# Banded attention into a softplus MLP on one core: q loaded as six tokens per partition, the picks and casts moved in the order of work

## The chip, the cores and the metric

The kernel runs on one core of one Trainium2 chip. The metric is the time of one execution on the device, in microseconds; the kernel before takes 512.18 us (median of three runs, 511.51 to 513.37).

The core's engines each run their own queue strictly in order: PE (matrix products), DVE and ACT (vector and scalar work; both read PE's results in PSUM), POOL (elementwise work that cannot read PSUM), and SP, which here only issues DMAs. An instruction waits at the head of its queue until what it needs is ready, and everything behind it waits too.

## The reference

Eight batches, eight heads, 576 tokens, head size 64. Attention with a band of 32 tokens to each side, plus eight global tokens that see everything and are seen by everyone; then an MLP with softplus.

```python
scores = scale * np.matmul(q, k.transpose(0, 1, 3, 2))
mask = np.abs(pos[:, None] - pos[None, :]) <= 32
mask = mask | is_global[:, None] | is_global[None, :]
attn = softmax(np.where(mask, scores, -1e9))          # over the last axis
x = np.matmul(attn, v)                                # -> (4608 tokens, 512)
out = softplus(x @ w_in) @ w_out                      # w_in 512 x 2048, w_out 2048 x 512
```

## The kernel before, in words

**Blocks and steps.** Heads go in pairs (p = 0 to 3), so that two heads of 64 fill 128 partitions. Queries go in blocks of 64 tokens: nine blocks a batch, 72 in all (n). A block's keys are the 128 positions around it and the eight global columns, 136 in all. The main loop runs over steps s; in step s the scores of block s are made, while older blocks are in later stages. Steps 0 to 9 ("P") hold attention alone. From step 10 on eight steps make a period: four "B" steps (s mod 8 = 2 to 5) carry the first MLP product h of 512 tokens, four products to each of 16 output tiles; four "A" steps carry the second product, o. Both are cut into four quarters a step (`moe(0)` to `moe(3)`), and attention work is put between the quarters. Tables filled ahead of the loop say which block is in which stage in which step: E (exponentials), M (sum and normalisation), TP (transpose of the probabilities), PGT (transpose of the global columns), VV (value product), TU (turns), CA (casts of q and k), SV (casts of v), G1 to G3 (rows of the global queries). The order in the code is the order in each queue; no planner changes it.

**One block.** `s_pe` (L344) makes scores in PSUM; `s_max` (L355, DVE) adds the mask, writes them to SBUF negated and takes the row's minimum; `s_sub` (L360, POOL) subtracts it; `expo` (L364, ACT); `total` (L368 to L371) sums on DVE, takes the reciprocal and, on POOL, multiplies by 0 for rows that are global queries; `norm` (L379, L380, POOL) multiplies the 512 band columns and the 32 global columns in two instructions; `pt_pe` and `pt_ev` (L387 to L395) transpose; `pg_pe` (L400, L403) transposes the global columns of four blocks at once and copies them into R; `v_pe` (L413, L415) multiplies by v and by the global rows and leaves the result in xT, half by DVE (L421) and half by ACT (L422).

**Turns.** q and k arrive with tokens on the partitions. POOL casts them to bf16 (`cast`, L234). A turn multiplies by a unit matrix on PE (L251), five products of 128 tokens and eight extra columns that pick the global tokens out, in two parts of three and two (SPLIT). ACT evicts q in two halves, one for each head (L261 for the first two batches, L264 after), into qz; DVE evicts k into kx (L271). Then the "picks": DVE reduces the global columns of q to qg (L267) and of k (L277, L278), and POOL copies the kx blocks that start at an odd 64 (L273, L274).

**Loads.** SP issues q, k and v through eight stage buffers, in the order in which they are cast; a cast gives its buffer to the next load. Each of q, k and v of a pair takes four DMAs in pieces of 256 bytes (L156, L161). vB is a copy of v moved by 64 tokens (L239, L240), also on SP's queue, as are the stores of the results (L447).

**Ahead of the loop** stand constants (identity, masks, one-hot rows; L173 to L221, L463 to L519), the turns of batch 0 and its global rows. One of the constants, the eight indices, is spread over the partitions by POOL (L189). POOL also issues the loads of the weights (L522, L524).

The products of block 0 need all turns of batch 0 and `globals1` to `globals3`; a turn needs its cast. In step s of the kernel before, casts are at the step's end, one step ahead of the turn.

Of the kernel before, what the change touches and what calls it, by code (L numbers as in the profile page):

```python
# [13 lines left out]
FP32 = mybir.dt.float32  # L14
# [4 lines left out]
def kernel(  # L19
# [24 lines left out]
    EXT = P + NG  # L44
    KD = d_model // P
# [21 lines left out]

    def bank(shape, dt, name):
        return psa.tile(shape, dt, tag="a", name=name)
# [5 lines left out]
    stage = [const([P, NT5, P], FP32, f"stage{i}") for i in range(NSTG)]  # L75
# [8 lines left out]
    R = [[const([P, P], BF16, f"R{i}_{j}") for j in range(NJ)] for i in range(2)]  # L84
# [36 lines left out]
    for b in range(1, B):  # L121
        lo = 9 * (b - 1)
        ok = [s for s in range(lo, lo + 9) if kind[s] == "B"][:HP] if b > 1 else [1, 3, 5, 7]
        for p, s in enumerate(ok):
            TU[s].append((b, p))
            CA[s - 1].append((b, p)) if s > 0 else None
# [7 lines left out]
        assert max(g2 + 1, vs + 1) <= vslot[9 * b]  # L134


    order = [(0, w, p) for p in range(HP) for w in range(2)] + [(0, 2, p) for p in range(HP)]
    for s in range(NS):
        order += [(b, w, p) for b, p in CA[s] for w in range(2)] + [(b, 2, p) for b in SV[s] for p in range(HP)]
# [4 lines left out]
    def load_next():  # L144
        if loaded[0] == len(order):
            return
        b, w, p = order[loaded[0]]
        st = stage[loaded[0] % NSTG]
        loaded[0] += 1
        src = (q, k, v)[w]  # L150
        off = 0 if w == 0 else WIN
        for t0, t1 in ((0, 1), (1, NT5 - 1), (NT5 - 1, NT5)):
            lo, hi = max(0, t0 * P - off), min(S, t1 * P - off)
            p0 = lo - (t0 * P - off)
            if t1 - t0 == 1:
                nc.sync.dma_start(  # L156
                    out=st[p0:p0 + hi - lo, t0, :].rearrange("p (h d) -> p h d", h=2),
                    in_=src[b, 2 * p:2 * p + 2, lo:hi, :].rearrange("h s d -> s h d"))
            else:
                for h in range(2):  # L160
                    nc.sync.dma_start(  # L161
                        out=st[:, t0:t1, h * D:(h + 1) * D],
                        in_=src[b, 2 * p + h, lo:hi, :].rearrange("(t s) d -> s t d", s=P))

    gi_dram = global_idx.rearrange("(n one) -> n one", one=1).bitcast(I32)
    gi = const([1, NG], I32, "gi")
# [8 lines left out]
    ident = const([P, P], FP32, "ident")  # L175
# [3 lines left out]
    def iota(shape, pattern, base, mult, name):  # L179
        i = const(shape, I32, name + "_i")  # L180
        G_.iota(i[:], pattern=pattern, base=base, channel_multiplier=mult)
        return i, const(shape, FP32, name)

    posA_i, posA = iota([P, NT5], [[P, NT5]], -WIN, 1, "posA")
    posQ_i, posQ = iota([P, NT5], [[P, NT5]], 0, 1, "posQ")
    gf1 = const([1, NG], FP32, "gf1")
    V_.tensor_copy(gf1[:], gi[:])
    gf = const([P, NG], FP32, "gf")
    G_.partition_broadcast(gf[:], gf1[:1, :], channels=P)  # L189
    lower = const([P, NG, NG], FP32, "lower")  # L190
# [9 lines left out]
    rhsQ = const([P, NT5, EXT], BF16, "rhsQ")  # L200
    for rhs in (rhsQ, rhsA):
        V_.tensor_copy(rhs[:, :, 0:P], ident[:].unsqueeze(1).to_broadcast([P, NT5, P]))

    hsel = const([P, 2], FP32, "hsel")
# [7 lines left out]
    same = const([P, NG, NG], FP32, "same")  # L212
# [3 lines left out]
    dup = const([P, NG], FP32, "dup")  # L216
    V_.reduce_max(out=dup[:], in_=same[:], axis=AX.X)
    gs = const([P, NG], FP32, "gs")
    V_.scalar_tensor_tensor(out=gs[:], in0=dup[:], scalar=16384.0, in1=gf[:], op0=OP.mult, op1=OP.add)
    for pos, rhs in ((posQ, rhsQ), (posA, rhsA)):  # L220
# [417 lines left out]
```

## Time and profile before

| | us |
|---|---|
| median of three runs | 512.18 |
| profiled execution | 508.42 |
| its span, first to last instruction | 506.7 |
| PE busy in the span | 388.2 |
| ACT / POOL / DVE busy | 311.9 / 286.7 / 251.1 |

A row of groups in the profile reads: line, engine, operation, what is written <- what is read, shape, count, then busy time in us and mean ns of one, then the idle time of the engine ahead of these instructions and what ended it. A row of waits reads: who waited <- for whom, total us, times, longest. A timeline row has start and duration in us, and in brackets the idle time just before. A number of us after a window (A:B) is the busy time of one engine in it.

### The profile page before, as it was taken

Reading aid. Unit: us, or ns where it says so; the run is one execution under the profiler, and the core shown is the slowest. Engines: PE = TensorE matmul, PEld = TensorE weight load, DVE = VectorE, ACT = ScalarE, POOL = GpSimd, SP = SyncE. Lnnn points to the kernel's source line nnn. Section 1 sums busy time; section 2 is a strip of 40 time slices with the busy share of each in tenths; the row PEclk is TensorE's granted clock in tenths of the full one; section 3 lists DMA queues with packets and bytes.
Section 4 is the critical chain, followed back from the end, with each engine's and each line's share of the span. In section 5 each row is a group of like instructions: output and inputs, shape, how many; then the busy total and the mean of one; then the engine's idle time right before and its main releaser. Section 6 shows DMA issues by size and latency. Waiting matters only on the chain.

```text
span 506.7 us, 8834 instructions
## 1 busy us (share of the span) xinstructions
PE 388.2 (77%) x2746; PEld 222.0 (44%) x2795; DVE 251.1 (50%) x1124; ACT 311.9 (62%) x628; POOL 286.7 (57%) x477
## 2 busy tenths in 40 slices
PE   0124445567987898789987979797979789999996
PEld 0112234434554455445544645463446345545542
DVE  3653745553664475447546645663465356526100
ACT  1242545467848675886876588476837685776741
POOL 1338885745595468559756853794279448437000
PEclk9999999599999999999999999898989899999999
DMA  4542997544246324441651364125512401101102
GB/s 105 131 108 64 206 208 150 128 114 100 63 114 152 88 55 115 130 96 43 167 125 49 85 159 96 42 68 133 119 43 66 111 1 43 43 1 41 43 7 77
DMA packets 125950, 46.72 MB, mean 92 GB/s; under 512 B 117712, under 2 KB 119760, under 8 KB 125904
## 3 DMA queue, kind: packets, MB, share of 16 engines
q1 hardware_dynamic: 123216, 41.97, 34.0%
q0 software_dynamic: 2688, 4.19, 4.5%
q8 instruction: 22, 0.36, 0.3%
q14 instruction: 24, 0.20, 0.1%
HBM read 36.70 MB, written 9.44 MB: 91 GB/s over the span
## 4 chain that ended last, share of the span: by engine, by line
PE 36%; POOL 16%; issue 13%; ACT 11%; DVE 9%; SPq 9%; DMA 5%; POOLq 1%; ACTq 0%
PE o L441 14%; PE h L433 10%; SPq L161 5%; SPq L156 4%; POOL st L360 3%; ACT qz L264 3%; PE xo L415 3%; PE xo L413 3%; POOL vA L231 3%; DVE st L355 3%; POOL qn L234 3%; ACT g L436 2%; DMA vB<-vA 2%; POOL pn L379 2%; PE pt L387 2%
## 5 line engine op out<-in xcount | busy, mean ns | idle before, releaser
L433 PE MATMUL h<-xT,win 128*128 128x512 bf16 x552 | 144.2, 387 | 8.0 <-ACT xT L422 6.3
L441 PE MATMUL o<-wout,g 128*128 128x512 bf16 x552 | 139.7, 384 | 1.2
L360 POOL TENSOR_TENSOR st<-st,nb 128x544 f32<-128x544 f32 x72 | 78.8, 1095 | 60.3 <-DVE nb L355 60.2
L436 ACT ACTIVATE g<-h 128x512 bf16<-128x512 f32 x144 | 82.7, 597 | 20.5 <-PE h L433 18.7
L355 DVE CUSTOM_DVE_ANT_0 st<-s,mask 128x136 f32<-128x136 f32 x288 | 68.7, 293 | 19.5 <-PE s L344 19.1
L379 POOL TENSOR_TENSOR pn<-st,rs 128x512 bf16<-128x512 f32 x72 | 74.8, 1039 | 6.0
L433 PEld LDWEIGHTS <-win 128*128 128x128 bf16 x576 | 53.6, 100 | 51.1 <-issue 10.4
L251 PE MATMUL turn<-rhsQ,qn 128*128 128x136 bf16 x160 | 21.8, 247 | 68.1 <-POOL qn L234 45.3
L441 PEld LDWEIGHTS <-g 128*128 128x128 bf16 x576 | 52.7, 99 | 44.0 <-issue 1.4
L273 POOL COPY kx<-kx 128x256 bf16<-128x256 bf16 x32 | 12.7, 397 | 95.6 <-DVE kx L271 95.6
L264 ACT CAST qz<-turn 64x408 bf16<-64x408 f32 (+1 forms) x96 | 51.0, 532 | 17.4 <-PE turn L251 16.9
L267 DVE TENSOR_REDUCE qg<-qz 128x16 bf16<-128x80 bf16 x32 | 9.5, 296 | 96.9 <-ACT qz L264 80.1
L368 DVE TENSOR_REDUCE sm<-st 128x4 f32<-128x544 f32 x72 | 51.2, 712 | 8.5 <-ACT st L364 8.0
L422 ACT CAST xT<-xo 64x256 bf16<-64x256 f32 x72 | 26.1, 367 | 44.6 <-DVE xT L421 42.6
L251 PEld LDWEIGHTS <-qn 128*128 128x128 bf16 x160 | 13.6, 107 | 85.8 <-POOL qn L234 75.7
L364 ACT ACTIVATE st<-st 128x544 f32<-128x544 f32 x72 | 44.6, 651 | 9.5 <-POOL st L360 9.2
L421 DVE CAST xT<-xo 64x256 bf16<-64x256 f32 x72 | 29.0, 413 | 28.3 <-PE xo L415 27.5
L413 PE MATMUL xo<-R,oz 128*128 128x128 bf16 x288 | 39.1, 228 | 4.9 <-ACT R L403 4.6
L387 PE MATMUL pt<-ident_b,pn 128*128 128x128 bf16 x288 | 30.1, 231 | 11.1 <-POOL pn L379 8.6
L261 ACT ACTIVATE qz<-turn,hrow 128x408 bf16<-128x408 f32 (+1 forms) x32 | 17.2, 634 | 28.2 <-PE turn L251 28.2
L344 PE MATMUL s<-kx,qz 128*128 128x136 bf16 x288 | 31.9, 234 | 1.2 <-ACT qz L261 0.6
L413 PEld LDWEIGHTS <-oz 128*128 128x128 bf16 x288 | 29.5, 103 | 5.1 <-DVE nb L355 1.3
(109 smaller groups left out, 567.2 us busy)
## 6 DMA issues: line engine op xcount, KB each, us to landing
out_dram<-osb SPq DMA_DIRECT2D x36, 256.0 KB, 2.0
stage<-in_q_dram SPq DMA_DIRECT2D x64, 96.0 KB, 2.4
stage<-in_k_dram SPq DMA_DIRECT2D x64, 96.0 KB, 2.3
stage<-in_v_dram SPq DMA_DIRECT2D x64, 96.0 KB, 2.4
vB<-vA SPq DMA_DIRECT2D x16, 256.0 KB, 3.8
stage<-in_k_dram SPq DMA_DIRECT2D x64, 48.0 KB, 2.1
stage<-in_v_dram SPq DMA_DIRECT2D x64, 48.0 KB, 2.1
stage<-in_q_dram SPq DMA_DIRECT2D x32, 64.0 KB, 2.0
```

The costliest lines, as they stand in the source:

```text
L251: nc.tensor.matmul(out=ps[:, t - t0, :], lhsT=c[:, t, :], rhs=rhs[:, t, :], start=True, stop=True)
L264: S_.copy(z[h * D:(h + 1) * D, t0:t0 + tn, :, h], ps[h * D:(h + 1) * D, 0:tn, :])
L355: V_.tensor_tensor_reduce(out=ST[n][:, p, :], in0=ps[:, y, :], in1=mask[:, n % NJ, :], scale=-SCALE, scalar=3.0e38, op0=OP.add, op1=OP.min ...
L360: G_.tensor_tensor(out=ST[n][:], in0=ST[n][:], in1=NB.pop(n)[:].unsqueeze(2).to_broadcast([P, HP, EXT]), op=OP.subtract)
L364: S_.activation(out=ST[n][:], in_=ST[n][:], func=AF.Exp, scale=-1.0)
L368: V_.reduce_sum(out=sm[:], in_=ST[n][:], axis=AX.X)
L379: G_.tensor_tensor(out=PN[n][:], in0=e[:, :, 0:P], in1=rs[:].unsqueeze(2).to_broadcast([P, HP, P]), op=OP.mult)
L387: nc.tensor.transpose(out=tp[:, p, :], in_=pn[:, p, :], identity=ident_b[:])
L413: nc.tensor.matmul(out=xo[:, p, :], lhsT=OVZ[b][:, p * P:(p + 1) * P], rhs=R[i][j][:, :], start=True, stop=False)
L433: nc.tensor.matmul(out=HB[0][:, :], lhsT=w_in_t[:, kd, kf * P:(kf + 1) * P], rhs=xT[t][:, kd, :], start=(kd == 0), stop=(kd == KD - 1))
L436: S_.activation(out=gt[t][:, kf, :], in_=HB[0][:, :], func=AF.Softplus)
L441: nc.tensor.matmul(out=HB[1][:, :], lhsT=gt[t][:, kf, ns * P:(ns + 1) * P], rhs=w_out_t[:, kf, :], start=(kf == 0), stop=(kf == KF - 1))
```

## The change

- **q** is loaded with one DMA for a pair: six consecutive tokens on each of 96 partitions, so that a piece is 1536 bytes. Six turning products of 96 rows and 104 columns, three in each half, then put columns in the order of the tokens through the address of the eviction (a step of 24 bytes). Each half's eviction is shared: the even head by ACT, the odd head by DVE.
- **k and v** take one DMA a head (two for a pair) and run over the head's ends into its neighbours; the first tile of the tensor and the last are cut. The stage memsets go. For batch 0, q is issued on ACT's queue.
- **The indices** come by a DMA that spreads them over the partitions; POOL's broadcast goes.
- **Picks** are put into a list and run in the next step behind the maxima. **Casts** of q and k go two steps ahead, and stand behind `s_sub`. v is cast a pair a step; `globals3` comes later with it.
- **norm** is one instruction over 544 columns; ACT copies the 128 global columns of four blocks together ahead of their transpose. The multiplication by 0 or 1 goes from POOL to DVE.
- **R** is one tile; the one-hot rows are made ahead of step 0, three to a copy. Start-up tiles share the space of g.
- **In a step** the transposes of all blocks come behind the first quarter, turns stand elsewhere (two parts ahead of the first quarter where the kind of step changes), and value products are all ahead of the last quarter.

```diff
+    NQ = 6
+    PQ = S // NQ
+    EXQ = PQ + NG
...
-    qz = [[const([P, NT5, EXT, 2], BF16, f"qz{i}_{p}") for p in range(HP)] for i in range(2)]
+    qz = [[const([P, NQ * EXQ, 2], BF16, f"qz{i}_{p}") for p in range(HP)] for i in range(2)]
...
-            CA[s - 1].append((b, p)) if s > 0 else None
+            CA[max(0, s - 2)].append((b, p))
...
-        vs = vslot[9 * (b - 1) - 1] if b > 1 else 6
-        SV[vs].append(b)
-        G3[max(g2 + 1, vs + 1)].append(b)
+        vs = vslot[9 * (b - 1) - 1] if b > 1 else 3
+        for p in range(HP):
+            SV[vs + 1 + p].append((b, p))
+        G3[max(g2 + 1, vs + 6)].append(b)
...
+        eng = nc.scalar if b == 0 and w == 0 else nc.sync
+        if w == 0:
+            eng.dma_start(
+                out=st[0:PQ, :].rearrange("p (h x) -> p h x", h=2),
+                in_=q[b, 2 * p:2 * p + 2, :, :].rearrange("h (p x) d -> p h (x d)", p=PQ))
+            return
...
+            eng.dma_start(out=o[:, t0:t1, :],
+                          in_=flat[r0 + t0 * P:r0 + t1 * P, :].rearrange("(t s) d -> s t d", s=P))
...
-    nc.sync.dma_start(out=gi[:, :], in_=gi_dram[:, 0:1].rearrange("n one -> one n"))
-    for s in stage:
-        V_.memset(s[0:WIN, 0, :], 0.0)
-        V_.memset(s[64:P, NT5 - 1, :], 0.0)
+    nc.scalar.dma_start(out=gi[:, :], in_=gi_dram[:, 0:1].rearrange("n one -> (one n)").partition_broadcast(P))
...
-    G_.partition_broadcast(gf[:], gf1[:1, :], channels=P)
...
+                c = sb.tile([P, NQ, P], BF16, tag="qn", name="qn", bufs=3)
+                G_.tensor_copy(c[0:PQ, :, :].rearrange("p s (h d) -> p s h d", h=2),
+                               st[0:PQ, :].rearrange("p (h s d) -> p s h d", h=2, s=NQ))
...
+            for t in range(NQ // 2):
+                nc.tensor.matmul(out=ps[:, t, :], lhsT=c[0:PQ, x * (NQ // 2) + t, :],
+                                 rhs=rhsQ[0:PQ, x * (NQ // 2) + t, :], start=True, stop=True)
...
-                    S_.copy(z[h * D:(h + 1) * D, t0:t0 + tn, :, h], ps[h * D:(h + 1) * D, 0:tn, :])
+            zx = z[:].rearrange("p (c s) h -> p s c h", s=NQ)[:, x * (NQ // 2):(x + 1) * (NQ // 2), :, :]
+            if b < 2:
+                S_.activation(out=zx[:, :, :, 0], in_=ps[:], func=AF.Copy, scale=hrow[:, 0:1])
+                V_.tensor_scalar(out=zx[:, :, :, 1], in0=ps[:], scalar1=hrow[:, 1:2], scalar2=None, op0=OP.mult)
+            else:
+                S_.copy(zx[0:D, :, :, 0], ps[0:D, :, :])
+                V_.tensor_copy(zx[D:P, :, :, 1], ps[D:P, :, :])
...
+            if x == 1:
+                after.append(pick_k)
+
+    def picks():
+        while after:
+            after.pop(0)()
...
-        G_.tensor_scalar(out=rs[:], in0=rs[:], scalar1=notg[:, n % NJ:n % NJ + 1], scalar2=None, op0=OP.mult)
+        V_.tensor_scalar(out=rs[:], in0=rs[:], scalar1=notg[:, n % NJ:n % NJ + 1], scalar2=None, op0=OP.mult)
...
-        G_.tensor_tensor(out=PN[n][:], in0=e[:, :, 0:P], in1=rs[:].unsqueeze(2).to_broadcast([P, HP, P]), op=OP.mult)
-        G_.tensor_tensor(out=GC[n // 4][:, n % 4, :, :], in0=e[:, :, P:EXT],
-                         in1=rs[:].unsqueeze(2).to_broadcast([P, HP, NG]), op=OP.mult)
+        PN[n] = GC[n // 4][:, n % 4, :, :]
+        G_.tensor_tensor(out=PN[n], in0=e[:], in1=rs[:].unsqueeze(2).to_broadcast([P, HP, EXT]), op=OP.mult)
...
+        S_.copy(gc[:], GC.pop(n4)[:, :, :, P:EXT].rearrange("p a b g -> p (a b) g"))
...
     for p in range(HP):
-        cast(0, 0, p)
-        cast(0, 1, p)
+        if p == 0:
+            for p_ in range(2):
+                cast(0, 1, p_)
+                cast(0, 0, p_)
+        elif p + 1 < HP:
+            cast(0, 1, p + 1)
+            cast(0, 0, p + 1)
         turn(0, p)
+        if p > 0:
+            after.pop(0)()
+            after.pop(0)()
...
+            V_.memset(R[64:P, :, :, :], 0.0)
+        tp = bank([64, 4, P], BF16, "oh")
...
+        for i in range(2):
+            S_.copy(R[0:64, i, j0:j1, :], tp[:, 0:j1 - j0, :])
...
-    one_hot_rows(0, 2)
+    picks()
     globals1(0)
     globals2(0)
     globals3(0)
+    for j in (0, 3, 6):
+        one_hot_rows(j, j + 3)
```

The body of a step after the change, from the scores on, with the lines that were moved (`first` is true where the kind of step differs from the one before; `turn_one` does the next of a pair's four parts, if one is left):

```python
        for x in range(2):
            if f is not None:
                s_pe(f, x)
                s_max(f, x)
        picks()
        if f is not None:
            s_sub(f)
        for b, p in CA[s]:
            cast(b, 0, p)
            cast(b, 1, p)
        if first:
            turn_one()
            turn_one()
        moe(0)
        for n in PGT[s]:
            pg_pe(n)
        for n in M[s][:1]:
            total(n)
            norm(n)
        for n in TP[s]:
            pt_pe(n)
            pt_ev(n)
        turn_one()
        moe(1)
        for n in VV[s][:2]:
            v_pe(n)
        for n in M[s][1:]:
            total(n)
            norm(n)
        turn_one()
        moe(2)
        for b in G1[s]:
            globals1(b)
        for b in G3[s]:
            globals3(b)
        for n in VV[s][2:]:
            v_pe(n)
        turn_one()
        turn_one()
        moe(3)
        for n in late[s]:
            expo(n)
        for b, p in SV[s]:
            cast(b, 2, p)
            if p == HP - 1:
                shift_v(b)
```

More of the change, by code (lines that the diff above doesn't have):

```diff
@@ L149, in load_next @@
         loaded[0] += 1
[L150 to L163, printed above, removed]
@@ L513, in one_hot_rows @@
             GL["ohn"] = ohn
+            V_.memset(R[64:P, :, :, :], 0.0)
+        tp = bank([64, 4, P], BF16, "oh")
         for j in range(j0, j1):
[L515 to L519 removed]
+            nc.tensor.transpose(out=tp[:, j - j0, :], in_=GL["ohn"][:, j, :, :, :], identity=ident_b[:])
+        for i in range(2):
+            S_.copy(R[0:64, i, j0:j1, :], tp[:, 0:j1 - j0, :])
     for i in range(KD):
```

197 lines of the change are left out of this document (104 added, 93 removed).

## The prediction

> **What bounds the kernel now.** First the page's head, busy times and chain of waits (what ended last).
>
> ```profile
> span 506.7 us, 8834 instructions
> PE 388.2 (77%) x2746; PEld 222.0 (44%) x2795; DVE 251.1 (50%) x1124; ACT 311.9 (62%) x628; POOL 286.7 (57%) x477
> ...
> PE 36%; POOL 16%; issue 13%; ACT 11%; DVE 9%; SPq 9%; DMA 5%; POOLq 1%; ACTq 0%
> ```
>
> No engine is full, and the chain changes engines all the time: the time is set by who waits for whom in queues that run in order. So I cut the span where the work changes: the first row subtraction of the attention (53.31), the first h product (102.71), and the h product of the last period (438.29). The view of busy time by stretch has, after the stretch and its length, the busy us of PE, weight load, DVE, ACT and POOL, then clock, DMA share and GB/s.
>
> ```profile
> 0.00:53.31 53.31, 12.62 (x70) 7.45 (x71) 27.02 (x121) 13.21 (x31) 23.69 (x50) 1.00 0.48 106
> 53.31:102.71 49.40, 24.47 (x187) 18.53 (x188) 28.07 (x135) 23.77 (x58) 36.57 (x60) 0.86 0.89 170
> 102.71:438.29 335.58, 288.94 (x2124) 164.59 (x2164) 180.21 (x803) 236.28 (x471) 209.28 (x342) 0.97 0.36 90
> 438.29:506.70 68.41, 62.16 (x366) 31.46 (x373) 15.80 (x70) 38.65 (x70) 17.12 (x27) 1.00 0.09 34
> ```
>
> In the first two stretches PE does 37 us of work in 102.7: they are lost to it. In the third, seven periods of 512 tokens, PE is busy 288.9 of 335.6, so 46.6 us are idle, and everything gained there is part of these. The waits of PE in the third stretch, then POOL's and DVE's longest in it (total, times, longest):
>
> ```profile
> PE turn L251 <- POOL qn L234: 22.8, 15, 2.3
> PE pt L387 <- POOL pn L379: 5.0, 3, 2.3
> PE h L433 <- ACT xT L422: 4.7, 7, 0.7
> PE ov L328 <- DVE lg L325: 4.1, 5, 2.5
> PE ov L328 <- POOL vA L231: 2.6, 2, 1.3
> PE pt L387 <- DVE nb L355: 1.9, 1, 1.9
> PE gt L400 <- POOL gc L380: 1.1, 2, 0.5
> ...
> POOL kx L273 <- DVE kx L271: 74.5, 24, 5.6
> ...
> DVE qg L267 <- ACT qz L264: 80.1, 24, 4.1
> ```
>
> The largest PE wait, 22.8, is for the cast of q. The cast is late because POOL, in order, stands at the copy of kx's odd blocks (74.5) until DVE has evicted k, and DVE stands at the reduction to qg (80.1) until ACT has evicted q. One turning step thus holds three engines, and the cast for the next is queued behind it.
>
> **The change part by part.** *Start.* POOL and DVE at the start:
>
> ```profile
> 7.90 0.28 POOL L189 PARTITION_BROADCAST gf<-gf  x1 [6.13 <-issue]
> ...
> 15.96 0.13 POOL L181 IOTA pidx_i<- 128x1 int32 x1 [7.30 <-DMA stage<-in_k_dram]
> ...
> 16.34 0.71 POOL L234 CAST qn<-stage 128x640 bf16<-128x640 f32 x1
> ...
> 17.05 0.75 DVE L213 TENSOR_TENSOR same<-gf 128x64 f32<-128x64 f32 x1
> ...
> 18.79 0.72 PE L251 MATMUL turn<-rhsQ,qn 128*128 128x136 bf16 x5 [18.79 <-DVE rhsQ L221]
> ...
> stage<-in_q_dram SPq DMA_DIRECT2D x64, 96.0 KB, 2.4
> ...
> 53.31 1.17 POOL L360 TENSOR_TENSOR st<-st,nb 128x544 f32<-128x544 f32 x1
> ...
> POOL kx L273 <- DVE kx L271: 14.8, 4, 5.0
> ```
>
> The two pauses of POOL, 6.13 and 7.30, stand on both sides of the one partition broadcast; I read them as its code coming in and the old one coming back. (A load named as releaser does not fit: iota reads none.) The change replaces the broadcast by a DMA that spreads the indices over the partitions. The indices are issued first on ACT's queue and land, by the 2.4 of a load, at about 4; that transfer of many tiny pieces is in no row, so between 4 and 8. Then "same" starts at 5.5 instead of 17.05: 11.5 earlier. The q loads go beside the indices on ACT's queue, which is empty then.
>
> From there to 53.31 POOL waits another 14.8 for kx (four times). The change defers the copies and reductions ("picks") by one pair, casts one pair ahead, and gives DVE half of each q eviction. POOL then has no wait that long, and DVE becomes the measure. Prices, one row each:
>
> ```profile
> L264 ACT CAST qz<-turn 64x408 bf16<-64x408 f32 x48 | 29.3, 610 | 17.2 <-PE turn L251 16.9
> L264 ACT CAST qz<-turn 64x272 bf16<-64x272 f32 x48 | 21.7, 453 | 0.3
> L271 DVE CAST kx<-turn 128x408 bf16<-128x408 f32 x32 | 18.3, 573 | 0.6 <-PE turn L251 0.5
> L271 DVE CAST kx<-turn 128x272 bf16<-128x272 f32 x32 | 13.8, 431 | 1.8 <-PE turn L251 1.8
> L360 POOL TENSOR_TENSOR st<-st,nb 128x544 f32<-128x544 f32 x72 | 78.8, 1095 | 60.3 <-DVE nb L355 60.2
> L379 POOL TENSOR_TENSOR pn<-st,rs 128x512 bf16<-128x512 f32 x72 | 74.8, 1039 | 6.0
> L371 POOL TENSOR_SCALAR rs<-rs,notg 128x4 f32<-128x4 f32 x72 | 21.3, 295 | 4.3 <-DVE rs L370 3.9
> L380 POOL TENSOR_TENSOR gc<-st,rs 128x32 bf16<-128x32 f32 x72 | 17.2, 239 | 0.0
> L234 POOL CAST qn<-stage 128x640 bf16<-128x640 f32 x32 | 23.1, 723 | 0.0
> L303 DVE TENSOR_SCALAR nb<-m 64x1 f32<-64x1 f32 x8 | 1.6, 205 | 0.3
> L403 ACT COPY R<-gt 32x128 bf16<-32x128 bf16 x72 | 18.4, 255 | 21.6 <-PE gt L400 20.4
> L518 DVE MEMSET R<- 64x64 uint32 x18 | 1.5, 112 | 0.3
> L519 ACT COPY R<-oh 64x128 bf16<-64x128 bf16 x18 | 3.4, 263 | 8.3 <-PE oh L516 8.3
> L436 ACT ACTIVATE g<-h 128x512 bf16<-128x512 f32 x144 | 82.7, 597 | 20.5 <-PE h L433 18.7
> ...
> ACT xT L422 <- DVE xT L421: 42.6, 37, 4.2
> ```
>
> A half now has 3 x 104 = 312 columns. Between 272 and 408 that is 473 ns on DVE and 499 on ACT. The write with a step of 24 bytes is in no row; it lies between the same price and, at worst, the 408-column one (573 and 610), and I take the same price. A pair costs DVE two halves more (0.95) and ACT, once two of its four copies are gone, 1.0 instead of 2 x (0.610 + 0.453) = 2.13.
>
> The one-hot rows, so far spread over the steps up to 2, now all stand before step 0. The 18 fills of R become one, of which 10 stood there already: 0.9 more for DVE at most. The 18 ACT copies become 6 of three times the size, 4.7 at most and 1.6 at least, behind the global rows where ACT has nothing else before step 1. Scratch in g's buffer costs nothing: its last reader ends long before the first h.
>
> DVE is busy 27.0 before 53.31; with eight halves (3.8) it needs 31 with no wait at all, a gain of 22. With the head start alone the gain is 11.5. The global rows' chain PE, DVE, ACT, DVE, PE before the first score stays as it was and cannot be hidden, so I take the middle, first subtraction at about 37: **-16** (-22 to -11.5).
>
> *Steps 0 to 9.* POOL loses the multiplication by notg (0.295, to DVE at about 0.205) and the second normalisation: 0.295 + 1.039 + 0.239 - 1.095 = 0.478 a block, 4.8 for ten. The q cast grows from 640 to 768 elements, by 0.145 at most (nothing at least), four times 0.6. POOL 36.6 becomes 32.4; DVE 28.1 + 3.8 + 2.1 becomes 34. So the stretch lies between 34, its fullest engine, and 49.4. The same transfers in less time raise the DMA share from 0.89 towards 1, though the eight stage buffers let loads lag; I take 41: **-8** (-15 to 0). The weights are issued as late in the order as before, ahead of the picks, and are wanted at the first h, about 40 us later.
>
> *The seven periods.* Casts stand two steps ahead of their turn and before the step's first products, and the kx copies in the next step behind the maxima, so POOL's wait of 74.5 has nothing left to wait for: the 22.8 go. The cover is POOL's room: 209.3 of 335.6 busy, less 0.478 x 56 blocks = 27. If it is gone, at most the 22.8 return. The v casts, one in each of four steps instead of four in a row, shorten the longest stay of POOL; shift_v then comes four steps later (batch 2: step 19 for 15), five before its first reader. The last value products now stand ahead of the last quarter of o, so xT is ready before h: the 4.7 go. Fewer stores into SP's line change nothing PE waits for here; of the loads, 12 issues of a pair become 5, with SP's stores and vB shift queued behind them, so these move earlier at no cost.
>
> Against it: the global columns are copied out by ACT first (nearest 0.255), and their transpose stands one quarter (4 products) earlier, so "gt" asks some 1.1 earlier for a normalisation that comes 2 x 0.478 earlier; between 0 and 1.1 a period, I take 0.3, +2. Two of the global products (steps 16 and 24) move to 21 and 29, among turns, where DVE is behind: from a mean of 0.8 to the longest, 2.5 (rows "ov"), so up to +3.4, I take +2. For DVE's new waits, below. The pt rows (6.9) and the rest stay. 22.8 + 4.7 - 4 = 23.5: **-24** (-42, when pt and ov go too, to -3, when what PE gets early is only late elsewhere). The last stretch has the same wait for xT at its two h products: **-1**.
>
> *Sum.* The profiled execution took 508.42, 1.7 more than its span. 508.4 - 16 - 8 - 24 - 1 = 459.4. The median of the runs is 512.18, 3.8 above this execution; I carry that over: **463**.
>
> **The rivals.** *(A) The waits come back on another engine.* For: ACT has 236 of 335.6 and DVE goes from 180 to about 180 + 56 x 0.473 + 56 x 0.205 = 218; against: each still has 30% room. Steady -8, steps 0 to 9 -5: 508.4 - 16 - 5 - 8 + 3.8 = 483 (474 to 491).
>
> *(B) All of it comes.* Every bound at its end: 508.4 - 22 - 15 - 42 - 1 + 3.8 = 432 (to 448). Against: the pt waits at the change from softplus to exp have a table load in front that is not touched.
>
> *(C) Slower: DVE is tied to ACT.* The q eviction's second half, on DVE, reads the same bank as ACT's half. The last row above shows what two engines do there: for xT, ACT waits for DVE's half to end, 42.6 us in all, though they read different partitions. So DVE's half stands behind ACT's half (0.499) and, at worst, a softplus (0.597); behind it on DVE are the k eviction, the sums and the next step's maxima, on which POOL waits. 64 halves x 1.1 = 70 if all is on the path: 533. It decides from 49/64 = 0.77 per half. Against: ACT loses 1.1 a pair, and DVE already stands 80.1 for ACT at qg.
> The Trainium skill, "PSUM — Partial Sum Buffer", section "PSUM bank collisions raise a hardware error", says that two engines may access one bank at once when they are in different quadrants of 32 partitions. By that rule 48 of the 64 halves (partitions 0 to 63 and 64 to 127; the other 16 read all) need no wait and (C) shrinks to 16 x 1.1 = 18, a gain still; the rows show the wait taken, and I keep (C) whole.
>
> *(D) The change doesn't do what it says:* a pause of POOL remains at the start, or the indices land late. Then 11.5 stay: 474.
>
> **How the numbers follow.** Forecast 0.56 (448 to 474), A 0.20, B 0.10, D 0.03, C 0.11. What this kernel's measurement can tell from no change is about 0.5%. C in full is slower, 0.08; C at its turning point is no change, 0.03; the rest, 0.89, is faster. The range 440 to 490 leaves out C, most of B's lower end and A's tail, about 0.18.
>
> **What would show it.** Start: no pause of POOL near 7 us, the first turn before 9. Steps: first subtraction near 37, first h near 79. Periods: no row of turn waiting for qn, POOL's kx wait under 10 us, seven periods in about 312. Wrong, if the first h is early but the periods are not shorter (A), or if DVE's wait for ACT at the q half exceeds 50 us (C).

## The result and the profile after

The changed kernel takes **566.6 us** (median), the kernel before 511.8 in the same comparison: a ratio of **1.108** (95% interval 1.102 to 1.113). It is slower, where 463 was forecast. The head of the page after, its busy times and its chain of waits:

```profile
span 565.1 us, 8490 instructions
PE 403.2 (71%) x2778; PEld 230.1 (41%) x2827; DVE 380.5 (67%) x1229; ACT 337.5 (60%) x570; POOL 258.9 (46%) x332
...
PE 33%; DVE 27%; ACT 22%; issue 6%; DMA 5%; POOL 5%; POOLq 0%; SPq 0%; ACTq 0%; DVEq 0%
```

POOL lost 28 us, as meant. DVE gained 129, and its share of the chain went from 9% to 27%. The view of busy time by stretch, cut at the same three marks as before (first row subtraction, first h, h of the last period):

```profile
0.00:55.95 55.95, 13.70 (x78) 7.84 (x79) 33.55 (x100) 17.27 (x19) 23.75 (x49) 1.00 0.65 127
55.95:113.54 57.59, 24.17 (x193) 19.69 (x193) 44.52 (x148) 26.76 (x45) 34.68 (x43) 0.76 0.80 161
113.54:495.24 381.70, 302.82 (x2142) 171.09 (x2182) 283.89 (x902) 254.03 (x435) 186.26 (x228) 0.93 0.30 78
495.24:565.10 69.86, 62.55 (x370) 31.45 (x374) 18.51 (x81) 39.47 (x73) 14.16 (x13) 0.99 0.09 35
```

The loss is in the seven periods (381.7 for 335.6) and in steps 0 to 9 (57.6 for 49.4); the start is 2.6 later instead of 16 earlier. In the seven periods DVE went from 180 to 284 where 218 was expected. The view of groups says which instructions these are:

```profile
L302 ACT CAST qz<-turn 64x312 bf16<-64x312 f32 x48 | 73.0, 1585 | 2.4 <-PE turn L282 2.4
L303 DVE CAST qz<-turn 64x312 bf16<-64x312 f32 x48 | 71.2, 1580 | 28.8 <-ACT qz L302 28.5
...
L421 DVE TENSOR_SCALAR rs<-rs,notg 128x4 f32<-128x4 f32 x72 | 25.7, 357 | 2.6
L320 DVE COPY kx<-g 128x72 bf16<-128x72 bf16 x32 | 24.8, 775 | 1.1
L299 ACT ACTIVATE qz<-turn,hrow 128x312 bf16<-128x312 f32 x16 | 24.6, 1727 | 9.4 <-PE turn L282 9.4
L300 DVE TENSOR_SCALAR qz<-turn,hrow 128x312 bf16<-128x312 f32 x16 | 23.9, 1620 | 8.9 <-ACT qz L299 8.9
```

A q half takes 1.58 us on either engine (1.62 and 1.73 in the first two batches), where I had priced 0.473 on DVE and 0.499 on ACT. Added up over 64 halves that is 71 us more on each. The waits of the whole span after (total, times, longest):

```profile
POOL kx L321 <- DVE kx L314: 101.9, 25, 7.4
...
PE gt L450 <- ACT gc L449: 41.2, 18, 4.7
...
DVE qz L303 <- ACT qz L302: 28.5, 22, 2.8
...
PE turn L282 <- POOL qn L261: 24.3, 3, 20.1
```

PE no longer waits for q's cast in the periods: of the 24.3 left, 20.1 are one wait at the start. But POOL's wait for the kx blocks is still there (101.9 in the span, 95.6 before), and PE has a new wait, 41.2 for the global columns. The timeline of the start, and the row of the indices' DMA (KB, us from issue to landing):

```profile
14.23 0.17 DVE L214 CAST scratch<-scratch 128x8 f32<-128x8 int32 x1 [13.24 <-DMA scratch<-in_global_idx_dram]
...
18.51 0.74 POOL L265 CAST kn<-stage 128x640 bf16<-128x640 f32 x1 [16.13 <-DMA stage<-in_k_dram]
...
20.08 0.70 PE L282 MATMUL turn<-rhsQ,qn 96*128 96x104 bf16 x6 [20.08 <-POOL qn L261]
```

```profile
scratch<-in_global_idx_dram ACTq DMA_DIRECT2D x1, 4.0 KB, 13.4
```

POOL's two pauses are gone, but 4 KB of indices land after 13.4 us, k's first load is late with them, and the first turn starts 1.3 later than before.

### The profile page after: what moved, and what is told of

It is laid out like the page before. It is cut to its first block, busy times and chain, and to the rows that moved or that the text cites. A ratio compares the mean times of both kernels' runs of the same rounds, so it can differ in the third digit from the quotient of the medians.

```text
span 565.1 us, 8490 instructions
## 1 busy us (share of the span) xinstructions
PE 403.2 (71%) x2778; PEld 230.1 (41%) x2827; DVE 380.5 (67%) x1229; ACT 337.5 (60%) x570; POOL 258.9 (46%) x332
## 4 chain that ended last, share of the span: by engine, by line
PE 33%; DVE 27%; ACT 22%; issue 6%; DMA 5%; POOL 5%; POOLq 0%; SPq 0%; ACTq 0%; DVEq 0%
PE o L491 12%; PE h L483 8%; ACT qz L302 8%; DVE qz L303 6%; ACT g L486 3%; DVE sm L418 3%; DVE kx L314 3%; DMA stage<-in_k_dram 3%; DVE st L405 3%; PE xo L463 3%; PE xo L465 3%; DVE kx L320 3%; DVE qz L300 3%; DMA stage<-in_v_dram 2%; PE pt L435 2%
## 5 line engine op out<-in xcount | busy, mean ns | idle before, releaser
L483 PE MATMUL h<-xT,win 128*128 128x512 bf16 x555 | 147.9, 393 | 13.5 <-ACT g L486 11.9
L486 ACT ACTIVATE g<-h 128x512 bf16<-128x512 f32 x144 | 93.5, 677 | 43.1 <-PE h L483 41.8
L429 POOL TENSOR_TENSOR pn<-st,rs 128x544 bf16<-128x544 f32 x72 | 78.6, 1091 | 70.9 <-DVE rs L421 46.9
L303 DVE CAST qz<-turn 64x312 bf16<-64x312 f32 x48 | 71.2, 1580 | 28.8 <-ACT qz L302 28.5
L483 PEld LDWEIGHTS <-win 128*128 128x128 bf16 x576 | 53.4, 100 | 60.2 <-issue 20.1
L302 ACT CAST qz<-turn 64x312 bf16<-64x312 f32 x48 | 73.0, 1585 | 2.4 <-PE turn L282 2.4
L321 POOL COPY kx<-kx 128x256 bf16<-128x256 bf16 x32 | 12.8, 401 | 102.0 <-DVE kx L314 101.9
L394 PE MATMUL s<-kx,qz 128*128 128x136 bf16 x288 | 35.5, 240 | 22.3 <-DVE qz L303 14.1
L282 PE MATMUL turn<-rhsQ,qn 96*128 96x104 bf16 x192 | 20.1, 231 | 36.5 <-POOL qn L261 24.3
L495 ACT COPY osb<-o 128x512 f32<-128x512 f32 x36 | 20.9, 581 | 36.8 <-PE o L491 29.7
L394 PEld LDWEIGHTS <-qz 128*128 128x128 bf16 x288 | 25.6, 106 | 41.2 <-issue 27.4
L435 PE MATMUL pt<-ident_b,pn 128*128 128x128 bf16 x288 | 28.5, 243 | 12.7 <-POOL pn L429 6.5
L282 PEld LDWEIGHTS <-qn 96*128 96x128 bf16 x192 | 15.5, 111 | 46.5 <-POOL qn L261 24.8
## 6 DMA issues: line engine op xcount, KB each, us to landing
win<-in_moe_w_in_dram POOLq DMA_DIRECT2D x4, 512.0 KB, 10.6
```

The lines of the kernel that those rows point to most:

```text
L302: S_.copy(zx[0:D, :, :, 0], ps[0:D, :, :])
L303: V_.tensor_copy(zx[D:P, :, :, 1], ps[D:P, :, :])
L394: nc.tensor.matmul(out=ps[:, y, :], lhsT=qz[i][p][:, j * G:(j + 1) * G, :], rhs=kx[i][p][:, j, :], start=True, stop=True)
L429: G_.tensor_tensor(out=PN[n], in0=e[:], in1=rs[:].unsqueeze(2).to_broadcast([P, HP, EXT]), op=OP.mult)
L483: nc.tensor.matmul(out=HB[0][:, :], lhsT=w_in_t[:, kd, kf * P:(kf + 1) * P], rhs=xT[t][:, kd, :], start=(kd == 0), stop=(kd == KD - 1))
L486: S_.activation(out=gt[t][:, kf, :], in_=HB[0][:, :], func=AF.Softplus)
```

## The experiments

The theories. **1**: the write with a step of 24 bytes is itself the price of the half. **2** (rival C): the half is slow because two engines share a bank, or through other traffic. **3**: the new order of work costs by itself. **4**: the indices' many small pieces hold up the loads at the start. **5** came later: small DVE instructions stand until POOL's instruction has ended. "Base" below is the changed kernel with q in tiles of 128 tokens and the indices in rows of 64 bytes.

| kernel | us | ratio to before, 95% | first subtraction | first h | seven periods |
|---|---|---|---|---|---|
| before | 511.8 | 1 | 53.3 | 102.7 | 335.6 |
| forecast | 463 | | 37 | 79 | 312 |
| changed | 566.6 | 1.102 to 1.113 | 56.0 | 113.5 | 381.7 |
| neighbours 4 bytes apart | 489.8 | 0.957 to 0.972 | 48.5 | 94.0 | 324.4 |
| loops exchanged | 506.0 | 0.994 to 1.002 | 50.2 | 98.8 | 335.5 |
| indices in 64-byte rows | 556.1 | 1.086 to 1.106 | 45.3 | 102.9 | 381.0 |
| base | 479.5 | 0.940 to 0.949 | 37.7 | 86.9 | 323.0 |
| base, late transpose and value products | 464.3 | 0.911 to 0.916 | 37.7 | 84.2 | 309.6 |
| base, late transpose only | 477.1 | 0.928 to 0.939 | 37.6 | 86.9 | 319.3 |
| base, spread on ACT | 484.3 | 0.950 to 0.955 | 37.5 | 83.7 | 329.1 |
| base, both halves on ACT | 489.8 | 0.959 to 0.966 | 37.7 | 86.4 | 332.7 |
| all repaired but the step | 538.7 | 1.050 to 1.063 | 45.3 | 101.1 | 366.2 |

The times are medians. Each ratio is to the kernel before as it ran in the same series: 511.8 beside the changed kernel, then 507.2 (the next three runs), 508.5 (the base, the 464.3, and the two that give ACT more) and 510.7 (the rest). So times of different series can be compared to about 1%, 5 us. The three marks are read from the profiled execution, which took 508.4 for the kernel before and 483.3 for the base, and lay within 2 us of the median for the others.

**The price of the step, alone.**

```diff
+    S_.copy(z[0:D, 0:624:2], lo)        # 4 bytes; then 0:1248:4, 0:1872:6, ... 0:9984:32
+    S_.copy(z6[0:D, 0:3, :, 0], lo3)    # the changed kernel's form
+    S_.copy(zc[0:D, :, 0:3, 0], lo3.rearrange("p s c -> p c s"))   # loops exchanged
```

> A price list, not the kernel: it leaves the whole computation out and does evictions alone, 64 partitions x 312 columns from one PSUM bank to bf16 in SBUF, six times each, first on ACT (partitions 0 to 63), then on DVE (64 to 127), with nothing beside them. Lines in order: write steps of 4, 8, 12, 16, 20, 24, 32 and 64 bytes, then the changed kernel's own form (3 rows of 104, step 24 bytes), then the same elements with the loops exchanged (104 groups of 3 neighbours 4 bytes apart). Theory 1 (the step of 24 bytes is itself the price): about 0.5 us at 4 bytes on both engines, as the rows of 64x272 and 64x408 of the kernel before say, and 1.5 to 1.6 us at 24 bytes and in the kernel's form, alone as in the kernel; the price rises between 4 and 24 bytes, and the exchanged loops come out between, 0.5 to 1.1 us. Theory 2 (my rival C, the two engines at one bank, or other traffic of the kernel): with nothing beside it the kernel's form takes 0.5 us whatever the step.

The groups, longest first. On ACT the steps of 4, 8, 12, 16 and 24 bytes are L54, L56, L58, L60 and L64, the kernel's form L70, the exchanged loops L72; L94 and L96 are the last two forms on DVE:

```profile
L94 DVE CAST z<-pb 64x312 bf16<-64x312 f32 x6 | 9.4, 1560 | 0.2
...
L60 ACT CAST z<-pa 64x312 bf16<-64x312 f32 x6 | 9.2, 1530 | 0.2
...
L70 ACT CAST z<-pa 64x312 bf16<-64x312 f32 x6 | 9.1, 1516 | 0.2
L64 ACT CAST z<-pa 64x312 bf16<-64x312 f32 x6 | 9.1, 1515 | 0.2
...
L58 ACT CAST z<-pa 64x312 bf16<-64x312 f32 x6 | 7.1, 1186 | 0.2
L96 DVE CAST z<-pb 64x312 bf16<-64x312 f32 x6 | 5.1, 852 | 0.2
...
L56 ACT CAST z<-pa 64x312 bf16<-64x312 f32 x6 | 5.1, 842 | 0.2
L72 ACT CAST z<-pa 64x312 bf16<-64x312 f32 x6 | 5.1, 842 | 0.2
...
L54 ACT CAST z<-pa 64x312 bf16<-64x312 f32 x6 | 3.0, 498 | 0.2
```

498, 842, 1186, 1530: each 4 bytes of step add exactly 344 ns, and from 16 bytes on nothing is added (1515 at 24). As the rise ends at 16 bytes, I take lines of 16 bytes: a step of 4, 8, 12 and 16 bytes makes 312 elements touch 78, 156, 234 and 312 of them, and 344 / 78 = 4.4 ns a line. The exchanged loops touch one line and a half for three neighbours, 156 in all, and cost what the 8-byte step costs; that they read PSUM with a step of 416 bytes adds nothing that shows. With nothing beside it the kernel's form takes 1.52 and 1.56 us: theory 2 falls as an explanation of the half's length.
The Trainium skill says in "SBUF — State Buffer", section "Specifications (TRN2)", that SBUF has lines of 16 bytes, that two hits a line are needed for full bandwidth, and that each crossing to a new line pays. The flat part from 16 bytes on agrees; that two hits are enough doesn't, since the 8-byte step has two a line and took 842 for 498.

**The step undone in the kernel.** The tokens of q stand in another order here, so the reordering is left out.

```diff
-            zx = z[:].rearrange("p (c s) h -> p s c h", s=NQ)[...]
+            zx = z[:].rearrange("p (s c) h -> p s c h", s=NQ)[...]
```

> The changed kernel with one thing undone: the two q halves are written in the order in which they stand in PSUM, neighbours 4 bytes apart instead of 24 (the tokens of q then stand in another order, so the reordering is left out of the computation; instructions, sizes, banks and waits are the same). Theory 1 (the price of the step): the halves fall from 1.58 to about 0.5 us, DVE gets back 64 x 1.1 = 70 us and ACT as much, and the time falls from 566 to 485 to 515, the rest against my forecast being the start (11.5) and small DVE work that got slower. Theory 2 (DVE tied to ACT at the bank): the wait of DVE's half for ACT's half stays near 28 us and the time above 540. Theory 3 (the new order of work costs by itself): halves short, but the time stays above 530.

489.8. The group's row and the stretch of the seven periods:

```profile
L303 DVE CAST qz<-turn 64x312 bf16<-64x312 f32 x48 | 23.9, 512 | 11.2 <-ACT qz L302 9.9
```

```profile
93.97:418.32 324.35, 290.96 (x2182) 168.90 (x2182) 241.01 (x902) 209.99 (x435) 186.28 (x228) 0.95 0.35 92
```

One address pattern was worth 77 us by the times, 73 by the ratios. Undoing it turned a kernel that is 11% slower into one that is 3.6% faster. Theory 3 does not explain the loss, though one piece of the new order costs about 15, as will be seen. The wait for ACT's half fell with the half, from 28.5 to 9.9. In the whole span DVE's busy time fell by 57 and ACT's by 59, less than the sum over the halves, as neighbouring records overlap (last section). PE's busy time in the periods fell too, from 302.8 to 291.0 at a granted clock of 0.93 and 0.95; why is not shown.

**The loops exchanged.** The same result in every element, three neighbours written together:

```diff
+            zx = z[:].rearrange("p (c s) h -> p c s h", s=NQ)[:, :, x * (NQ // 2):(x + 1) * (NQ // 2), :]
+            ps = ps[:].rearrange("p s c -> p c s")
```

> The changed kernel with the loops of the q eviction exchanged: for each of the 104 columns the three neighbouring tokens are written 4 bytes apart (the columns then 24 bytes apart), and PSUM is read with a step of 416 bytes; the result is the same in every element. Theory 1 in the form that each new stretch of SBUF costs, however few bytes of it are used: three elements share one, a half takes 0.5 to 0.9 us, and the time is within 20 us of the run with the plain order. Theory 1 in the form that it is the 24 byte step in any loop: the half stays at 1.5 us and the time at 560 to 570. Theory 2 (the tie): as for the plain order, above 540.

The half took 867 ns on DVE and 860 on ACT, and the kernel 506.0, no different from before. The three kernels stand in the order of their half length, but not on a straight line: 0.51, 0.87 and 1.58 us give 489.8, 506.0 and 566.6, so the first 0.36 costs 16 and the next 0.71 costs 61. That fits DVE having no room left at the upper end, which is argued, not shown.

**The indices.**

```diff
-    gi = temp([P, NG], I32, "gi")
-    ... in_=gi_dram[:, 0:1].rearrange("n one -> (one n)").partition_broadcast(P))
+    gi = temp([P, NG, 2], I32, "gi")
+    ... in_=gi_dram.rearrange("n w -> (n w)").partition_broadcast(P))
```

> The changed kernel with one thing changed at the start: the indices are spread over the 128 partitions as whole rows of 64 bytes (both words of each index, 128 pieces) instead of 1024 pieces of 4 bytes; DVE then converts every second word. Theory 4 (the many small pieces hold the DMA engines up for some 10 us at the start): landing falls from 13.4 to 3 to 5 us, the first k cast starts at 8 to 10 instead of 18.5, the first turn at 10 to 12 instead of 20.1, and the time falls by 5 to 11 us, to 555 to 562. If the number of pieces doesn't matter, the indices land after 13 us again and the time stays at 566.

```profile
scratch<-in_global_idx_dram ACTq DMA_DIRECT2D x1, 8.0 KB, 3.4
```

```profile
9.48 0.70 PE L282 MATMUL turn<-rhsQ,qn 96*128 96x104 bf16 x6 [9.48 <-POOL qn L261]
```

Twice the bytes land in a quarter of the time; the first turn starts 10.6 earlier and the kernel takes 10.5 less. The first h comes 10.6 earlier as well, and the periods are as long as before (381.0 for 381.7). Number and size of the pieces were changed together, so which of the two counts stays open.

**Both repairs with every element right.** q goes back to tiles of 128 tokens and five products; all else of the change stays.

```diff
-    qz = [[const([P, NQ * EXQ, 2], BF16, ...
+    qz = [[const([P, NT5, EXT, 2], BF16, ...
-        if w == 0:
-            eng.dma_start(out=st[0:PQ, :]..., in_=q[b, 2 * p:2 * p + 2, :, :].rearrange("h (p x) d -> p h (x d)", p=PQ))
-            return
-        flat = (k, v)[w - 1]...
+        off = 0 if w == 0 else WIN
+        flat = (q, k, v)[w]...
```

> The changed kernel with both repairs at once, and every element right: q is kept as 128 tokens per tile as in the kernel before (one DMA per head over the flattened rows, as the change does for k and v), so that an evicted half is written with neighbours 4 bytes apart, and the indices come as rows of 64 bytes. All else of the change stays: order of work, casts two steps ahead, halves on ACT and DVE, the merged normalisation. Theory 1 with theory 4: the gains add, 489.8 (plain order) less 10.5 (rows of 64 bytes) = 479, 474 to 485. If the larger q loads were worth something by themselves, their loss shows as a time above 485.

479.5, where 479 was the sum. The larger q loads were worth nothing that shows here. What PE still waits for most, in the stretch of the seven periods of this kernel, and the timeline of one such place:

```profile
PE gt L436 <- ACT gc L435: 26.6, 14, 4.3
```

```profile
341.02 1.09 POOL L415 TENSOR_TENSOR pn<-st,rs 128x544 bf16<-128x544 f32 x1 [0.17 <-DVE rs L407]
...
342.15 0.30 ACT L435 COPY gc<-pn 128x128 bf16<-128x128 bf16 x1 [1.70 <-POOL pn L415]
...
342.50 0.23 PE L436 MATMUL gt<-ident_b,gc 128*128 128x128 bf16 x1 [3.82 <-ACT gc L435]
```

POOL's normalisation of the group's fourth block ends at 342.1, ACT copies its global columns, and PE has stood 3.8 us. This is the first of a period's two; the second costs about 0.4 each time.

**The transpose and the value products one quarter later.**

```diff
         for n in PGT[s]:
-            pg_pe(n)
+            pg_gc(n)                  # ACT's copy stays here
...
         moe(1)
-        for n in VV[s][:2]:
-            v_pe(n)
+        for n in PGT[s]:
+            pg_pe(n)
...
         moe(2)
+        for n in VV[s][:2]:
+            v_pe(n)
```

> The run before, with the transpose of the global columns and the first two value products of a step put one quarter later, where the kernel before had them; ACT's copy of the columns stays where it is. In the run with the plain order PE waited 37.5 us for that copy (18 times). If those waits are on the path (I had priced them at 2 us): the wait falls under 15 us, and the time by 8 to 20, to 460 to 472. If they only stand in front of another wait: the time stays within 4 of the run before, with PE's wait for xT or for h's bank in their place.

464.3, ratio 0.913. The stretches:

```profile
0.00:37.66 37.66, 14.56 (x75) 7.74 (x75) 26.64 (x100) 9.87 (x19) 23.28 (x49) 1.00 1.02 182
37.66:84.17 46.51, 24.49 (x187) 19.34 (x188) 37.20 (x148) 19.52 (x45) 34.04 (x43) 1.00 1.19 215
84.17:393.75 309.58, 286.01 (x2160) 165.48 (x2159) 241.88 (x902) 208.81 (x435) 184.38 (x228) 0.98 0.40 99
393.75:462.10 68.35, 62.74 (x377) 31.48 (x374) 18.45 (x81) 39.36 (x73) 14.19 (x13) 1.00 0.10 35
```

PE is now busy 286.0 of 309.6 in the periods, and the granted clock there is 0.98 (0.93 in the changed kernel).

**The transpose alone.** As above, without moving the value products.

> The base with q as 128 tokens and rows of 64 bytes (479.5), with the transpose of the global columns alone one quarter later; the two value products stay where the change put them, now right behind the transpose, so they need its copies to R at once. If PE's wait for ACT's copy was the whole loss: 464 to 468, as with both. If the value products must move too, PE waits for the copies to R instead: 472 to 482.

477.1: only 2.4 of the 15.2 (by the ratios, which allow for the series, about 5 of 16). With no other work between them, PE waits in small steps for the copies into R:

```profile
PE xo L455 <- ACT R L445: 7.2, 17, 1.1
```

That is 7.2 us in the span, where the run before had 1.4, and no other new wait of PE's is above 0.3. In the seven periods the two kernels differ by 9.7: PE is idle for 5.0 more, which is the part of this wait that lies there, and busy for 4.8 more, at a granted clock of 0.97 against 0.98. Why it is busy longer stays open. That most of the gain needs both moves is shown.

**The spread of the picked columns on ACT.**

```diff
-                V_.tensor_copy(z[:, :, P:EXT], g8[:].unsqueeze(1).to_broadcast([P, NJ, NG]))
+                S_.copy(z[:, :, P:EXT], g8[:].unsqueeze(1).to_broadcast([P, NJ, NG]))
```

> The same base (q as 128 tokens, rows of 64 bytes) with one instruction moved: the spread of the picked columns over the blocks of kx, 32 of 128x72, goes from DVE to ACT. In the changed kernel it took 775 ns on DVE against 203 in the kernel before. If DVE is what POOL and PE wait for in the turning steps: DVE loses 25 us, ACT gains 32 x 0.25 = 8, and the time falls by 4 to 10, to 469 to 475. If DVE has room there by now: no change, 477 to 481.

484.3, about 5 slower than the base, which neither expectation had. DVE lost the 26 us, but ACT, in order, now stands for DVE's pick, and DVE's q half in turn for ACT:

```profile
ACT kx L306 <- DVE g L305: 42.9, 25, 3.8
...
DVE qz L289 <- ACT qz L288: 33.2, 42, 1.8
```

In the base the latter was 9.6. By these rows, work moved to a free engine cost more in its queue than it saved.

**Both halves on ACT** (batches 2 to 7).

```diff
-                V_.tensor_copy(zx[D:P, :, :, 1], ps[D:P, :, :])
+                S_.copy(zx[D:P, :, :, 1], ps[D:P, :, :])
```

> The same base with both halves of q's eviction of batches 2 to 7 on ACT, as in the kernel before (DVE's half of the first two batches stays). It asks what the tie of rival C is worth at the low price: DVE loses 48 x 0.5 = 24 us of work and the wait for ACT at the half (9.9 in the run with the plain order), ACT gains 24. If the tie holds the steps up, the time falls by 4 to 10 us; if giving DVE the half was a gain, as I had assumed, it rises by 3 to 10; within 3, neither.

489.8, 10 slower than the base. Giving DVE a half is a gain at the low price, tie and all.

**Everything repaired but the step.** The changed kernel with rows of 64 bytes and the late transpose and value products.

> The changed kernel as it is (6 tokens per partition, write step of 24 bytes), with the two other repairs: indices as rows of 64 bytes, and the transpose of the global columns with the value products behind it one quarter later. What is left against the 464.3 of the run with all three repairs is the price of the step. If the three terms add: 566.6 less 10.5 less 15.2 = 541 (534 to 548), so a step price of about 77. If the late transpose helps only where DVE has room (with the step DVE is the bound): 552 to 557.

538.7. Against 464.3 the step costs 74.4 on the best base; from the other side it cost 76.8. The three terms add: 566.6 - 10.5 - 76.8 - 15.2 = 464.1, for 464.3 measured. That is closer than times from different series can be trusted; the sum without the step, 540.9, lies 2.2 from the 538.7 of this run.

**The spread on POOL, then the product with notg as a product of two tensors.** Both on top of the 464.3.

```diff
-                V_.tensor_copy(z[:, :, P:EXT], g8[:]...)
+                G_.tensor_copy(z[:, :, P:EXT], g8[:]...)
```

```diff
-        V_.tensor_scalar(out=rs[:], in0=rs[:], scalar1=notg[:, n % NJ:n % NJ + 1], scalar2=None, op0=OP.mult)
+        V_.tensor_tensor(out=rs[:], in0=rs[:], in1=notg[:, n % NJ:n % NJ + 1].to_broadcast([P, HP]), op=OP.mult)
```

> The run with all repairs (464.3), with the spread of the picked columns over kx (32 of 128x72) on POOL, directly ahead of POOL's own two copies, instead of on DVE. There it took 842 ns on DVE, 0.90 to 1.14 us wherever POOL was in its row subtraction of 1.09 us, 0.18 to 0.28 beside POOL's copies and casts. Theory 5 (DVE's copy stands until POOL's subtraction has ended): on POOL it takes 0.2 to 0.4 us, DVE loses 27 us of busy time, and the time falls by 0 to 6, since DVE has room by now (70%). If the copy is slow for its shape, it is slow on POOL too (0.8 and more), and the time rises by up to 5.

> The run before, with the product of the reciprocals and notg (128x4, 72 times, 391 ns in the run with all repairs) written as a product of two tensors instead of a tensor with a scalar: same engine, same elements, same result. With POOL idle the tensor-scalar form took 0.23 us, beside POOL's subtraction 0.32 to 0.83, at the start of POOL's product 1.11; the reciprocal just ahead of it took 0.18 always. Theory 5 in the narrow form (only some forms of instruction on DVE stand for POOL): the product of tensors takes about 0.18 to 0.25 always, DVE loses about 11 us, the time falls by 0 to 3. If any instruction there stands for POOL: again 0.35 to 0.4.

466.3 (0.908 to 0.919) and 463.6 (0.904 to 0.915): neither can be told from 464.3. On POOL the spread takes 259 ns, so its shape is not slow; the periods stay at 309.0 though DVE is busy for 21 less in them. The product of tensors takes 384 ns on average, against 391 for the product with a scalar in the 464.3 run: the form of theory 5 in which only the product with a scalar stands for POOL falls.

```profile
L306 POOL COPY kx<-g 128x72 bf16<-128x72 bf16 x32 | 8.3, 259 | 63.1 <-DVE g L305 59.4 <-DMA stage<-in_k_dram 2.2 <-DMA stage<-in_q_dram 1.5
```

```profile
L407 DVE TENSOR_TENSOR rs<-rs,notg 128x4 f32<-128x4 f32 x72 | 27.7, 384 | 2.5
```

## Why the prediction was wrong

**The reading of what bounds the kernel was right.** The 22.8 of PE's wait for q's cast went, and h's wait for xT too: no such row stands among PE's waits of the changed kernel's periods. With the three repairs, which leave the casts and picks where the change put them and give up the larger q loads, the first subtraction stands at 37.7 for 37 and the periods take 309.6 for 312; PE is idle in them for 23.6, where it was 46.6. What each part of the new order gave by itself is not shown, but for the shared halves (about 10). That 464.3 lies so near 463 is partly luck: profile against profile it is 463.9 for 459.4, as steps 0 to 9 took 46.5 for 41, and the 3.8 that I carried over to the median did not come again (0.3).

**The step that failed: the price of the q half.** I wrote that the write with a step of 24 bytes was in no row and lay "between the same price and, at worst, the 408-column one". Both ends came from rows whose step was 2 or 4 bytes, so they bounded the number of columns and not the step. The half costs 1.58 us, 1.1 more, 64 times on each of two engines. It costs 1.52 and 1.56 with nothing beside it, and undoing the step alone brings the half to 0.51 and gives the 77 back. ACT's and DVE's shares of the chain went from 11% and 9% to 22% and 27%. Worth 73 to 77 us of the 104 missed.

**One sign was set wrong.** I wanted POOL's kx wait under 10 in the periods. The row of the changed kernel's periods, then that of the kernel with all repairs:

```profile
POOL kx L321 <- DVE kx L314: 78.9, 18, 7.4
```

```profile
POOL kx L307 <- DVE kx L300: 32.7, 18, 4.5
```

So the deferred copies still wait for DVE, and the kernel that meets the forecast has 32.7 of the 74.5 left. The mark did not tell what it was meant to tell.

**The term "gt", +2.** I had the transpose asking 1.1 earlier at most for a normalisation that comes 0.96 earlier. The first transpose of a period asks 1.9 to 4.3 us too early, because the group's fourth normalisation stands behind its own sums on DVE and its exponential on ACT. Measured with the value products it belongs to: 15.2 (16 by the ratios).

**The indices "between 4 and 8".** They landed after 13.4, and what lies behind them on the DMA engines was late too: 10.5. This is the second half of rival D ("or the indices land late"), with the 11.5 that I gave it. POOL's two pauses did go with the broadcast; that they were code coming in and out is not shown.

**Rival C** had the sign and, by chance, the size (1.1 us for each of 64 halves) with the wrong mechanism. The wait of DVE's half for ACT's is there, but it is 28.5 and 8.9, under the 50 that I had set as its mark, and it falls with the half. By the rule weighed there (the Trainium skill, "PSUM — Partial Sum Buffer", section "PSUM bank collisions raise a hardware error") the 28.5 need not be; the kernel takes that wait all the same, and no run here drops it. **Rival A**'s 483 is near the 479.5 of the base, but for the sake of "gt", not of a busy engine; its 218 for DVE counts 56 halves in the periods, which hold 48. **Rival B** didn't show.

**Smaller terms.** The product with notg was priced at 205 and took 357; the spread, which I had not priced as it only moved, went from 203 to 775: it moved from beside POOL's copies of 0.40 to beside its subtraction of 1.09. Neither decides: taken off DVE or put in another form they gained nothing.

## What to carry to other kernels

A price for an instruction belongs to its address pattern as much as to its element count: when an edit puts a reordering into a write, price the lines it touches, and if no row has that step, leave the upper end of the range open or measure it alone. When work is asked for earlier, walk back the whole chain of what it needs; when the transposes were moved, their users had to move with them. An edit that is nearly right can look altogether wrong: three local faults hid a gain of 9%.

## What the runs showed of the hardware

**Lines.** An eviction of 312 columns to SBUF pays 4.4 ns for every 16-byte line it touches, up to one line per element, on ACT and DVE alike (498 to 1530 and 508 to 1539 ns from 4 to 16 bytes of step), measured with nothing beside it.

**A longer record is not always a higher price.** In the changed kernel the record of a softplus directly behind a q half is 0.92 long (20 of them, 0.74 to 0.97), against 0.56 to 0.60 for those that stand singly in the timeline and not behind a half. The timeline of ACT, and then that of the run with neighbours 4 bytes apart:

```profile
128.45 1.56 ACT L302 CAST qz<-turn 64x312 bf16<-64x312 f32 x1
129.51 0.92 ACT L486 ACTIVATE g<-h 128x512 bf16<-128x512 f32 x1
130.33 1.52 ACT L302 CAST qz<-turn 64x312 bf16<-64x312 f32 x1
```

```profile
107.18 0.50 ACT L302 CAST qz<-turn 64x312 bf16<-64x312 f32 x1
...
108.18 0.49 ACT L302 CAST qz<-turn 64x312 bf16<-64x312 f32 x1
```

The softplus's record starts at 129.51, while the half's ends at 130.01: the two overlap by 0.50. From one half's start to the next, with one softplus between, pass 1.88 here and 1.00 with the short half. So the pair is 0.88 longer, less than the 1.06 of the half alone, and the softplus adds no price of its own.

**DVE stands for POOL, for some instructions.** In the run with all repairs:

```profile
97.37 1.09 POOL L396 TENSOR_TENSOR st<-st,nb 128x544 f32<-128x544 f32 x1
...
97.66 0.84 DVE L306 COPY kx<-g 128x72 bf16<-128x72 bf16 x1
```

```profile
L406 DVE RECIPROCAL rs<-sm x56: 177/178/180, 87.3 to 389.8; 128x4 f32<-128x4 f32 x56
L407 DVE TENSOR_SCALAR rs<-rs,notg x56: 229/315/1115, 87.5 to 390.0; 128x4 f32<-128x4 f32 x56
```

The copy ends at 98.50, just behind POOL's subtraction at 98.46. With POOL at its kx copies it takes 0.18, but these are only 0.40 long, and whether it stood for one of them can't be told. The product of four numbers takes between 229 and 1115 ns (least, median, most), the reciprocal ahead of it 178 always. The Trainium skill, "SBUF — State Buffer", section "🔬 SBUF: two separate sides", has one pair of ports that DVE and POOL lock for a whole instruction, taken by DVE's fast forms and by those with two inputs from SBUF. The copy, both products (the one of two tensors takes 161 to 1123) and the unharmed reciprocal agree with that, if the copy and the product with a scalar run in a fast form, which no run here shows.

**Small pieces.** The queue of the indices and of batch 0's q, by packets, MB and share, in the changed kernel and then with rows of 64 bytes:

```profile
q10 hardware_dynamic: 1872, 1.18, 1.0%
```

```profile
q10 hardware_dynamic: 976, 1.19, 0.9%
```

896 packets fewer are the 1024 pieces that became 128; the landing went from 13.4 to 3.4 us. The Trainium skill's "DMA: Bandwidth & Descriptors", section "🎯 Rules for kernel authors", says that a last dimension with a step becomes one descriptor per element; the packets agree.
